# Attention and two feed-forward layers in one kernel: the first four tiles' probabilities transposed on TensorE, their swapped queries copied by ScalarE, and the row factors' Newton steps gathered

## The chip, the cores and the metric

One core of a Trainium2 chip runs the whole program. The metric is the device time of one execution in microseconds. The program before was run three times: 841.93, 842.92 and 845.69 us, so the median is 842.92 us.

## The reference, cut to what matters

```python
def _attn_ref(q, k, v):              # 4 batches, 8 heads, 576 rows, 64 columns
    scores = scale * np.matmul(q, k.transpose(0, 1, 3, 2))
    mask = block_i >= block_j        # blocks of 64 rows
    scores = np.where(mask, scores, -1000000000.0)
    scores = scores - np.max(scores, axis=-1, keepdims=True)
    attn = np.exp(scores)
    attn = attn / (np.sum(attn, axis=-1, keepdims=True) + 1e-09)
    return np.matmul(attn, v)

def _moe_ref(x, g_ln, w_ch1, w_ch2): # x: 2304 rows of 512; hidden width 2048
    xn = (x - mu) / np.sqrt(var + 1e-06) * g_ln
    return x + np.maximum(xn @ w_ch1, 0.0) @ w_ch2

def _moe2_ref(x, w_gate, w_local, w1, w2):   # 8 experts, hidden width 1024
    logits = np.einsum('bsd,de->bse', x, w_gate)
    ...                              # one expert e for each row, p its softmax
    out[b, s] = p[e] * (np.maximum(x[b, s] @ w1[e], 0.0) @ w2[e])
```

w_ch1 and w_ch2 arrive as 64-bit numbers and are read as pairs of 32-bit integers.

## The kernel before, in words

The 2304 rows are 18 tiles of 128. Every product of 32-bit numbers is made of 16-bit parts, a high and a low one, so that each product is three 16-bit matmuls. The program has two halves. The first, up to some 625 us, runs the attention and the first feed-forward layer together; the second routes the rows to experts and runs the expert layer, 26 slots of some 10 us. The change is in the first half, and there in the part up to some 160 us.

**A step** is one head of one tile (18 x 8 = 144 steps, the loop at the end of the first half). For a step, `qk` makes the scores on TensorE (L308), `maxes` takes their negated row maximum on VectorE (L328, L332), and `exps` lets ScalarE take the exponential (L339) and cast its high part (L348), lets GpSimd subtract for the low part (L351), and has the pair of parts, called ph, transposed into pt by a DMA that SyncE's queue issues (L355). Four steps later `pv` multiplies pt with the values on TensorE (L370, L374), and ScalarE and VectorE bring the sums out (L382, L383). Tiles 0 and 1 have so few keys that two heads share one ph. Before a tile's steps its keys and queries are split in two parts and transposed by DMA (L247, L237). Of the queries a second copy with its two 64-row halves swapped is made by VectorE (L238, L239, one copy for each half); the second half of each score needs it.

**The weights** of the first layer are 32 pieces of 512 KB. VectorE makes a 32-bit float of a piece in three integer operations (`w_bits`, L195, L199, L202), ScalarE scales it and casts its high part (`w_hi`, L215, L216), GpSimd subtracts for the low part (`w_lo`, L220). Three buffers hold raw pieces. The first three loads are issued on SyncE's queue; every later one is issued on ScalarE's own queue (L181), behind the work that stands there. A piece's load is asked for when the piece three before it has been read.

**After a tile's last head**, `finish` divides, takes mean and variance (L395 to L418), makes a rough inverse root y on VectorE, normalises with it, splits and transposes the result by DMA into xg, and refines the row's factor by two Newton steps, seven small VectorE operations on one column (L436 to L455, with one column for each tile). The factor is only needed when `post` (L501) brings a tile out of the layer. `l1` multiplies xg with the first weights (L473 to L475) and brings the hidden columns out by ScalarE and VectorE (L477, L478); `l2` multiplies these with the second weights (L495 to L497). The first tile's `l2` needs all 32 pieces of the weights.

**What sets the order.** The program is written step by step. A scheduler then orders the instructions of the first half with a timeline of its own, so that an engine's order is not the order of the code. Code under `first(i)` gets a high priority for tiles below HT = 2. Each engine then works strictly in its order.

## Time and profile before

| what | us |
|---|---|
| median of three runs | 842.92 |
| the profiled execution's own time | 843.15 |
| its span from first to last instruction | 841.4 |
| TensorE busy with matmuls | 707.7 (84% of the span) |
| VectorE busy | 460.1 (55%) |
| ScalarE busy | 362.1 (43%) |
| GpSimd busy | 327.8 (39%) |

The shares are means over a program with different limits in its parts. In the first 160 us TensorE is idle more than half the time and VectorE hardly ever; from 280 us on it is the other way round. So a change in the first part is read from the rows of that part, in windows, and by who waits for whom there.

### The profile page before, as it was taken

The numbers are of one execution on the slowest core, as the hardware profiler recorded it, in microseconds if no ns is written. First come the engines' busy times: TensorE is split into PE (matmuls) and PEld (weight loads), VectorE is DVE, ScalarE is ACT, GpSimd is POOL, SyncE is SP. The second block draws the span as 40 slices with busy tenths as digits, with TensorE's granted clock in tenths as the row PEclk, the third lists the DMA queues.
The fourth block names the chain that finished last, engine by engine and source line by source line (L and its number), as shares of the span: only waits on it lengthen the run. The fifth ranks groups of instructions, "written<-read, shape, count | busy, mean of one in ns | idle before, by whom it ended". The sixth has DMA issues, their size and how long they took to land. (4 is left out here: it accounts for less than half of the span.)

```text
span 841.4 us, 16461 instructions
## 1 busy us (share of the span) xinstructions
PE 707.7 (84%) x5526; PEld 425.4 (51%) x5526; DVE 460.1 (55%) x1248; ACT 362.1 (43%) x843; POOL 327.8 (39%) x364
## 2 busy tenths in 40 slices
PE   0214758789899999898998999998997999999995
PEld 0113645486756857655654565555452444444442
DVE  2999979887755556765564575276881111111110
ACT  2764657675555437555553464164041111111110
POOL 1577747776465235454444553210002122112210
PEclk9999989999999999999999999999998999999999
DMA  9998998799987677799967865397116655665673
GB/s 193 194 227 203 210 203 196 147 184 178 168 144 157 132 141 153 123 184 173 166 131 132 170 100 102 65 341 253 40 43 127 112 125 126 125 121 130 132 129 73
DMA packets 328942, 127.33 MB, mean 151 GB/s; under 512 B 296912, under 2 KB 315344, under 8 KB 328848
## 3 DMA queue, kind: packets, MB, share of 16 engines
q1 hardware_dynamic: 321472, 100.73, 63.0%
q10 hardware_dynamic: 4176, 15.21, 6.8%
q0 software_dynamic: 3200, 10.23, 3.7%
q8 instruction: 48, 0.79, 0.4%
q14 instruction: 46, 0.38, 0.2%
HBM read 128.73 MB, written 9.70 MB: 165 GB/s over the span
## 5 line engine op out<-in xcount | busy, mean ns | idle before, releaser
L473 PE MATMUL dps<-xg,wide 128*128 128x128 f16 (+2 forms) x576 | 156.4, 282 | 28.0 <-DVE htl L478 14.8
L351 POOL TENSOR_TENSOR ph<-sm,ph 128x512 f16<-128x512 f32 (+6 forms) x120 | 132.2, 1105 | 121.8 <-ACT ph L348 83.9
L474 PE MATMUL dps<-xg,wide 128*128 128x128 f16 (+2 forms) x576 | 156.7, 282 | 0.0
L475 PE MATMUL dps<-xg,wide 128*128 128x128 f16 (+2 forms) x576 | 156.6, 282 | 0.0
L339 ACT ACTIVATE sm<-sm,sums 128x128 f32<-128x128 f32 (+8 forms) x144 | 87.9, 611 | 111.5 <-DVE sums L332 100.7
L308 PE MATMUL ps_s<-wide 128*128 128x128 f16 (+4 forms) x560 | 74.9, 260 | 49.2 <-DVE sums L328 27.4
L1001 DVE SCALAR_TENSOR_TENSOR hth<-hps,hth 128x512 f16<-128x512 f32 x38 | 26.2, 691 | 164.6 <-ACT hth L1000 164.4
L495 PE MATMUL dps<-wide,hth 128*128 128x512 f16 x288 | 110.8, 386 | 0.2 <-DVE early L564 0.2
L496 PE MATMUL dps<-wide,hth 128*128 128x512 f16 x288 | 110.7, 385 | 0.0
L497 PE MATMUL dps<-wide,htl 128*128 128x512 f16 x288 | 110.4, 383 | 0.0
L370 PE MATMUL ps_o<-wide,pt 128*128 128x128 f16 x464 | 59.3, 225 | 29.3 <-DVE ob L383 19.0
L474 PEld LDWEIGHTS <-wide 128*128 128x128 f16 x576 | 58.9, 102 | 47.1 <-issue 33.8
L478 DVE SCALAR_TENSOR_TENSOR htl<-dps,hth 128x128 f16<-128x128 f32 (+2 forms) x144 | 59.1, 417 | 42.2 <-ACT hth L477 41.7
L1025 POOL DMA_INDIRECT out<-eo,dst_i x19 | 19.2, 1013 | 156.1 <-ACT eo L1024 151.4
L328 DVE CUSTOM_DVE_ANT_0 sm<-ps_s,mask_a 128x256 f32<-128x256 f32 (+7 forms) x128 | 64.2, 516 | 18.2 <-POOL ph L351 9.6
L308 PEld LDWEIGHTS <-wide 128*128 128x128 f16 x560 | 39.6, 101 | 61.8 <-issue 27.3
L348 ACT CAST ph<-sm 128x512 f16<-128x512 f32 (+6 forms) x120 | 68.2, 570 | 1.6
L477 ACT ACTIVATE hth<-dps 128x128 f16<-128x128 f32 (+2 forms) x144 | 53.5, 375 | 33.5 <-PE dps L475 33.3
L475 PEld LDWEIGHTS <-wide 128*128 128x128 f16 x576 | 59.1, 103 | 14.8
L473 PEld LDWEIGHTS <-wide 128*128 128x128 f16 x576 | 59.1, 103 | 14.6 <-issue 0.6
L370 PEld LDWEIGHTS <-pt 128*128 128x128 f16 x464 | 43.7, 100 | 26.3 <-DMA pt<-ph 17.9
L374 PE MATMUL ps_o<-wide,pt 128*128 128x64 f16 x464 | 55.9, 197 | 0.0
(255 smaller groups left out, 1408.4 us busy)
## 6 DMA issues: line engine op xcount, KB each, us to landing
raws<-in_moe_w SPq DMA_DIRECT2D x38, 2048.0 KB
wraw<-in_moe_w_ch ACTq DMA_DIRECT2D x29, 512.0 KB
raws<-in_moe_w SPq DMA_DIRECT2D x24, 512.0 KB
rows<-x2h SPq DMA_DIRECT2D x18, 256.0 KB
raw<-in_k SPq DMA_DIRECT2D x32, 128.0 KB
raw<-in_q SPq DMA_DIRECT2D x32, 128.0 KB
raw<-in_v SPq DMA_DIRECT2D x32, 128.0 KB
pt<-ph SPq DMA_TRANSPOSE x120
```

The source lines that it names most:

```text
L308: nc.tensor.matmul(sp[:, a * P + o:b * P], lhsT=qt[i, part].rearrange("p (x t) c -> p x (t c)", t=2)[:, x, z::2], rhs=rhs, start=part == 0 ...
L328: nc.vector.tensor_tensor_reduce(out=sm[:, lo:n], in0=sp[:, lo:n], in1=mask[:, 5 * P - n + lo:5 * P], scale=-0.125, scalar=3.0e38, op0=ALU ...
L339: nc.scalar.activation(out=e, in_=e, func=AF.Exp, scale=-1.0, bias=sv[:, 0, h:h + 1], accum_out=sv[:, 1, h:h + 1],)
L348: nc.scalar.copy(out=ph4[:, :, 0, lo:], in_=sm[:, :, lo:])
L351: nc.gpsimd.tensor_tensor(out=ph4[:, :, 1, lo:], in0=sm[:, :, lo:], in1=ph4[:, :, 0, lo:], op=ALU.subtract)
L370: nc.tensor.matmul(o, lhsT=t[:, c], rhs=vt[kk][:, h].rearrange("p e d -> p (e d)"), start=c == 0, stop=False,)
L473: nc.tensor.matmul(hp, lhsT=wh, rhs=xg[g][:, kk], start=kk == 0, stop=False)
L474: nc.tensor.matmul(hp, lhsT=wh, rhs=xg[g][:, KD + kk], start=False, stop=False)
L475: nc.tensor.matmul(hp, lhsT=wl, rhs=xg[g][:, kk], start=False, stop=kk == KD - 1)
L495: nc.tensor.matmul(op[j], lhsT=hh, rhs=w2h[:, f], start=f == 0, stop=False)
L496: nc.tensor.matmul(op[j], lhsT=hh, rhs=w2l[:, f], start=False, stop=False)
L497: nc.tensor.matmul(op[j], lhsT=hl, rhs=w2h[:, f], start=False, stop=f == KF - 1)
```

## The change

Three things, all in the first half:

1. For tiles 0 to 3 (FEW = 4), except their last two steps, ph is no longer transposed by DMA. TensorE multiplies each 128 x 128 block of it with an identity matrix into PSUM, and ScalarE copies the result into pt (`emit_turns`, two steps behind the exponential). For this the score tiles of these four tiles take half the PSUM they had (512 columns), and two PSUM tiles for the transposes stand beside them.
2. For the same tiles ScalarE makes the swapped copies of the queries.
3. A tile's product w = y·var·y is put into a column of `roots`; the other Newton steps run later for all the columns that are there (`newton`, when a tile's `l2` is at its third quarter), and are told to stand behind the last weights' piece. The two operations that multiplied by a pointer scalar and a tensor become two plain products each.

Besides, HT is 4, so tiles 0 to 3 and their splits run at high priority, and the splits' buffers are two, with one of its own for xh.

```diff
-HT = 2
+HT = 4
+FEW = 4
+LAGT = 2
...
+    ident16 = const.tile([P, P], F16, name="ident16")
+    gp.affine_select(
+        out=ident16, in_=c_one16, pattern=[[1, P]], compare_op=ALU.is_equal, fill=0.0,
+        base=0, channel_multiplier=-1,
+    )
...
+    sctx["p"] = sctx["c"].enter_context(tc.tile_pool(name="ps_e", bufs=1, space=PSUM))
...
-        n = at.tile([P, H, 2, D], F16, tag="nat", name="qn", bufs=3)
+        n = at.tile([P, H, 2, D], F16, tag="nat", name="qn", bufs=2)
...
-        nc.vector.tensor_copy(b[0:D], a[D:P])
-        nc.vector.tensor_copy(b[D:P], a[0:D])
+        copy = nc.scalar.copy if i < FEW else nc.vector.tensor_copy
+        copy(b[0:D], a[D:P])
+        copy(b[D:P], a[0:D])
...
-            sps[i] = ps_a.tile([P, 1024], F32, tag="s", name="ps_s", bufs=2)
+            n = 1024 if i >= FEW else 512
+            sps[i] = sctx["p"].tile([P, n], F32, tag="s", name="ps_s", bufs=2)
...
-        nc.sync.dma_start_transpose(out=t[:, :2 * m * n // P], in_=ph[:, :2 * m * n])
+        if step[0] < FEW * H - 2:
+            turns.append((step[0], ph, t, 2 * m * n // P))
+        else:
+            nc.sync.dma_start_transpose(out=t[:, :2 * m * n // P], in_=ph[:, :2 * m * n])
...
+    def emit_turns(upto):
+        while turns and turns[0][0] <= upto:
+            _, ph, t, n = turns.pop(0)
+            tp = sctx["p"].tile([P, 8, P], F16, tag="t", name="ps_t", bufs=2)
+            for c in range(n):
+                nc.tensor.transpose(tp[:, c], ph[:, c * P:(c + 1) * P], ident16)
+            nc.scalar.copy(out=t[:, :n], in_=tp[:, :n])
...
-        xh = at.tile([P, 2, DM], F16, tag="nat", name="xh", bufs=3)
+        xh = at.tile([P, 2, DM], F16, tag="xh", name="xh", bufs=1)
...
-        f = fac[:, i:i + 1]
         nc.vector.scalar_tensor_tensor(
-            out=w, in0=y, scalar=var, in1=y, op0=ALU.mult, op1=ALU.mult
+            out=roots[:, 0, i:i + 1], in0=y, scalar=var, in1=y, op0=ALU.mult, op1=ALU.mult
         )
+        fresh_roots.append(i)
...
+    def newton():
+        if fresh_roots:
+            with tc.issue_after(piece[0].ins):
+                newton_steps()
...
+    def newton_steps():
+        a, b = fresh_roots[0], fresh_roots[-1] + 1
+        fresh_roots.clear()
+        f, w, y = fac[:, a:b], roots[:, 0, a:b], roots[:, 1, a:b]
+        tt = nc.vector.tensor_tensor
         nc.vector.tensor_scalar(
             out=f, in0=w, scalar1=-1.0, scalar2=3.0, op0=ALU.mult, op1=ALU.add
         )
-        nc.vector.scalar_tensor_tensor(
-            out=y, in0=f, scalar=w, in1=f, op0=ALU.mult, op1=ALU.mult
-        )
+        tt(out=y, in0=f, in1=w, op=ALU.mult)
+        tt(out=y, in0=y, in1=f, op=ALU.mult)
...
     def l2(g, j, c):
...
+        if c == 2 and g < len(GROUPS) - 1:
+            newton()
...
+                if steps[s + 1:s + 2] == [(FEW, 0)]:
+                    emit_turns(s)
+                    sctx["c"].close()
+                    sctx["p"] = actx.enter_context(tc.tile_pool(name="ps_s", bufs=1, space=PSUM))
...
+                with first(nx):
+                    if h == SK:
+                        split_k(nx, nc.gpsimd)
...
+        emit_turns(s - LAGT)
         emit_pv(s - (LAG if s < LATE else LAG + MPT))
```

The change also moves instructions. Three places, each engine's order before and now (line numbers are those of the kernel that is shown):

ScalarE at the start of the program, before. The casts of tile 0's keys and queries (L245, L230) are followed at once by the first weights' piece (L215, L216) and the load that it frees (L181).

```order
L245 CAST kn<-raw 128x8x64
L230 CAST qn<-raw 128x8x64
L215 ACTIVATE wide<-wide,gs 128x512
L216 CAST wide<-wide 128x512
L181 DMA wraw<-in_moe_w_ch 128x1024
L256 ACTIVATE wide<-raw 128x8x64
L245 CAST kn<-raw 128x8x64
L230 CAST qn<-raw 128x8x64
```

The same place now (in the changed kernel the weights' piece is L229, L230, its load L194, and the swapped copies are L253, L254).

```order
L260 CAST kn<-raw 128x8x64
L244 CAST qn<-raw 128x8x64
L253 COPY wide<-wide 64x1024
L254 COPY wide<-wide 64x1024
L229 ACTIVATE wide<-wide,gs 128x512
L260 CAST kn<-raw 128x8x64
L244 CAST qn<-raw 128x8x64
L230 CAST wide<-wide 128x512
L194 DMA wraw<-in_moe_w_ch 128x1024
```

The two swapped copies, which need the transposed queries, and the casts of tile 1 now stand ahead of the first load that ScalarE issues.

VectorE at the last pieces of the weights, before: a Newton chain (L442 to L455) stands between the last pieces.

```order
L442 SCALAR_TENSOR_TENSOR lns<-fac,lns 128x1
L328 ISA sm,sums<-ps_s,mask_a 128x512
L328 ISA sums 128x1
L202 SCALAR_TENSOR_TENSOR wt<-wraw,wt 128x512
L445 SCALAR_TENSOR_TENSOR fac<-lns,fac 128x1
L332 TENSOR_SCALAR sums<-sums 128x1
L448 SCALAR_TENSOR_TENSOR lns<-fac,lns 128x1
L451 TENSOR_SCALAR lns<-lns 128x1
L455 TENSOR_TENSOR fac<-fac,lns 128x1
L383 TENSOR_TENSOR ob<-ps_o,ob 128x256
```

The same place now: from the very last piece (its last operation is L216 here) on, towards the first tile that leaves the layer (L544, four rows further down).

```order
L216 SCALAR_TENSOR_TENSOR wt<-wraw,wt 128x512
L482 TENSOR_SCALAR fac<-roots 128x2
L519 SCALAR_TENSOR_TENSOR htl<-dps,hth 128x128
L492 TENSOR_SCALAR roots<-roots 128x1
L344 ISA sm,sums<-ps_s,mask_a 128x512
L344 ISA sums 128x1
L348 TENSOR_SCALAR sums<-sums 128x1
L485 TENSOR_TENSOR roots<-fac,roots 128x2
L496 TENSOR_TENSOR fac<-fac,roots 128x1
```

Two chains, one of tile 0 alone and one of tiles 1 and 2, have taken the place of three; the first begins ahead of the last piece, the second behind it. Up to that first tile VectorE has made the row maxima of 35 heads before and of 32 now, and four of the swapped half copies where there were twelve.

TensorE, now: the first transposes (L385) stand among the scores (L324) of tiles 0 and 1; before there is nothing between the scores there.

```order
L324 MATMUL ps_s<-wide 128x128
L385 LDWEIGHTS ph
L385 MATMUL ps_t<-ident_64,ph 128x128
L385 LDWEIGHTS ph
L385 MATMUL ps_t<-ident_64,ph 128x128
L385 LDWEIGHTS ph
L385 MATMUL ps_t<-ident_64,ph 128x128
L385 LDWEIGHTS ph
L385 MATMUL ps_t<-ident_64,ph 128x128
L385 LDWEIGHTS ph
L385 MATMUL ps_t<-ident_64,ph 128x128
L324 LDWEIGHTS wide
```

In all there are 144 transposes, all ahead of the first tile's logits, and 22 copies of them on ScalarE (4 of 512 columns, 8 of 768, 10 of 1024). Ahead of these logits TensorE had made 96 matmuls of scores and 190 of `pv` before, and makes 76 and 160 now; from the third tile's logits on the same counts stand ahead of each tile's as before, but for the transposes. On SyncE's queue the 22 transposes by DMA are gone.

## Rows read from the trace of the kernel before

**Rows 1.** Windows: busy time of each engine in stretches of the span (us, and in brackets how many instructions), then the granted TensorE clock, the DMA engines' busy share and GB/s. 162 us is where the first tile leaves the first layer, 203 us the third. The columns are PE, PEld (the weight loads), DVE, ACT, POOL.

```profile
0.00:20.00 20.00, 0.39 (x2) 0.13 (x2) 5.13 (x15) 4.58 (x7) 3.56 (x11) 1.00 0.92 189
...
20.00:62.00 42.00, 9.30 (x62) 6.35 (x63) 41.27 (x100) 27.62 (x69) 26.52 (x21) 1.00 0.97 212
...
20.00:162.00 142.00, 76.85 (x713) 54.49 (x713) 134.49 (x300) 87.40 (x213) 93.04 (x72) 0.96 0.94 200
162.00:203.00 41.00, 35.48 (x473) 27.33 (x472) 31.20 (x110) 29.13 (x82) 30.48 (x37) 0.96 1.02 177
...
260.00:320.00 60.00, 57.81 (x557) 41.57 (x555) 34.25 (x111) 28.94 (x83) 21.41 (x22) 1.00 0.68 135
```

**Rows 2.** Waits of VectorE from 20 to 158 us: who it waited for, us in total, times, longest.

```profile
DVE wt L195 <- DMA wraw<-in_moe_w_ch: 2.3, 2, 1.3
DVE htl L478 <- ACT hth L477: 1.9, 2, 1.5
DVE wide L238 <- DMA wide<-qn: 0.9, 1, 0.9
```

**Rows 3.** Timeline of VectorE (start, duration, us): the last operation on the last piece of the weights, and the first tile leaving the layer (`post`).

```profile
157.41 0.69 DVE L202 SCALAR_TENSOR_TENSOR wt<-wraw,wt 128x512 int32<-128x512 int32 x1
...
162.14 0.75 DVE L501 SCALAR_TENSOR_TENSOR x<-dps,fac,x 128x512 f32<-128x512 f32 x1 [1.12 <-PE dps L497]
```

**Rows 4.** Groups of VectorE's instructions from 20 to 162 us (count; busy us, mean ns of one; idle before): the swapped copies of six tiles and the factor chains of three.

```profile
L239 DVE COPY wide<-wide 64x1024 f16<-64x1024 f16 x6 | 4.9, 810 | 0.1
L238 DVE COPY wide<-wide 64x1024 f16<-64x1024 f16 x6 | 4.8, 805 | 1.0 <-DMA wide<-qn 0.9
L448 DVE SCALAR_TENSOR_TENSOR lns<-fac,lns 128x1 f32<-128x1 f32 x3 | 3.3, 1095 | 0.0
L445 DVE SCALAR_TENSOR_TENSOR fac<-lns,fac 128x1 f32<-128x1 f32 x3 | 2.9, 962 | 0.0
L442 DVE SCALAR_TENSOR_TENSOR lns<-fac,lns 128x1 f32<-128x1 f32 x3 | 2.4, 804 | 0.0
L436 DVE SCALAR_TENSOR_TENSOR lns<-lns 128x1 f32<-128x1 f32 x3 | 1.6, 526 | 0.0
L455 DVE TENSOR_TENSOR fac<-fac,lns 128x1 f32<-128x1 f32 x3 | 1.4, 474 | 0.0
L451 DVE TENSOR_SCALAR lns<-lns 128x1 f32<-128x1 f32 x3 | 0.4, 145 | 0.0
L439 DVE TENSOR_SCALAR fac<-lns 128x1 f32<-128x1 f32 x3 | 0.4, 139 | 0.0
```

**Rows 5.** Timeline of VectorE: the same operation in its short and its long form (swapped copy, chain product, last product), and two row maxima of a tile with 640 keys in succession.

```profile
20.34 0.42 DVE L239 COPY wide<-wide 64x1024 f16<-64x1024 f16 x1
...
80.87 1.28 DVE L239 COPY wide<-wide 64x1024 f16<-64x1024 f16 x1
...
88.58 0.21 DVE L442 SCALAR_TENSOR_TENSOR lns<-fac,lns 128x1 f32<-128x1 f32 x1
...
95.24 1.11 DVE L455 TENSOR_TENSOR fac<-fac,lns 128x1 f32<-128x1 f32 x1
...
147.01 1.10 DVE L442 SCALAR_TENSOR_TENSOR lns<-fac,lns 128x1 f32<-128x1 f32 x1
...
152.13 0.16 DVE L455 TENSOR_TENSOR fac<-fac,lns 128x1 f32<-128x1 f32 x1
...
158.14 0.77 DVE L328 CUSTOM_DVE_ANT_0 sm<-ps_s,mask_m 128x640 f32<-128x640 f32 x1
...
159.07 0.82 DVE L328 CUSTOM_DVE_ANT_0 sm<-ps_s,mask_m 128x640 f32<-128x640 f32 x1
```

**Rows 6.** Groups of ScalarE's instructions up to 180 us: casts of 512 and of 640 columns, and copies out of PSUM of 128 and of 256 columns.

```profile
L477 ACT ACTIVATE hth<-dps 128x128 f16<-128x128 f32 x38 | 10.2, 270 | 7.2 <-PE dps L475 7.2
...
L348 ACT CAST ph<-sm 128x512 f16<-128x512 f32 x12 | 7.3, 610 | 0.0
...
L348 ACT CAST ph<-sm 128x640 f16<-128x640 f32 x8 | 5.8, 720 | 0.1
...
L382 ACT COPY ob<-ps_o 128x256 f32<-128x256 f32 x9 | 3.2, 360 | 0.1
```

**Rows 7.** Waits of ScalarE from 20 to 62 us, in the same form as rows 2.

```profile
ACT wide L215 <- DVE wide L202: 8.7, 6, 4.0
ACT kn L245 <- DMA raw<-in_k: 8.0, 1, 8.0
ACT sm L339 <- DVE sums L332: 4.8, 5, 1.7
```

**Rows 8.** Timeline of ScalarE's sequencer: the first load of a weights' piece that it issues.

```profile
8.85 0.44 ACTq L181 DMA_DIRECT2D wraw<-in_moe_w_ch  x1
```

**Rows 9.** SyncE's DMA queue from 20 to 130 us: packets, MB, share of the 16 DMA engines' time.

```profile
q1 hardware_dynamic: 36286, 9.93, 54.6%
```

**Rows 10.** Timeline of TensorE: two pairs of matmuls of 128 columns in succession, one pair early and one later.

```profile
71.00 0.31 PE L475 MATMUL dps<-xg,wide 128*128 128x128 f16 x1
71.11 0.31 PE L473 MATMUL dps<-xg,wide 128*128 128x128 f16 x1
...
88.62 0.22 PE L473 MATMUL dps<-xg,wide 128*128 128x128 f16 x1
88.67 0.22 PE L474 MATMUL dps<-xg,wide 128*128 128x128 f16 x1
```

More of the change, by code (lines that the diff above doesn't have):

```diff
@@ L125 @@
     fac = wp.tile([P, NTILE], F32, name="fac")
+    roots = wp.tile([P, 2, NTILE], F32, name="roots")
     gs = wp.tile([P, KD], F32, name="gs")
@@ L132 @@
     ps_a = actx.enter_context(tc.tile_pool(name="ps_a", bufs=1, space=PSUM))
+    sctx = {"c": ExitStack()}
+    sctx["p"] = sctx["c"].enter_context(tc.tile_pool(name="ps_e", bufs=1, space=PSUM))
     wctx = {"c": ExitStack()}
@@ L184 @@
     wt = {}
+    piece = [None]
     def w_bits(p):
@@ L201, in w_bits @@
         )
-        nc.vector.scalar_tensor_tensor(
+        piece[0] = nc.vector.scalar_tensor_tensor(
             out=t, in0=low, scalar=29, in1=t, op0=ALU.logical_shift_right, op1=ALU.bitwise_or
@@ L243, in split_k @@
         r = raw.pop(("k", i))
-        n = at.tile([P, H, 2, D], F16, tag="nat", name="kn", bufs=3)
+        n = at.tile([P, H, 2, D], F16, tag="nat", name="kn", bufs=2)
         nc.scalar.copy(out=n[:, :, 0], in_=r)
@@ L354, in exps @@
         t = ring("pt", [P, 10, P], F16, LAG, MPT)
-        nc.sync.dma_start_transpose(out=t[:, :2 * m * n // P], in_=ph[:, :2 * m * n])
+        if step[0] < FEW * H - 2:
+            turns.append((step[0], ph, t, 2 * m * n // P))
+        else:
+            nc.sync.dma_start_transpose(out=t[:, :2 * m * n // P], in_=ph[:, :2 * m * n])
         for j in range(m):
             ptr[i, h - m + 1 + j] = t[:, 2 * n // P * j:2 * n // P * (j + 1)]
+    turns = []
+    def emit_turns(upto):
[5 more added lines that the diff above has]
+            nc.scalar.copy(out=t[:, :n], in_=tp[:, :n])
     obs = {}
@@ L406, in finish @@
         sm = at.tile([P, 12], F32, tag="lns", name="lns", bufs=2)
-        mean, var, y, w = (sm[:, c:c + 1] for c in (6, 7, 8, 9))
+        mean, var, y = (sm[:, c:c + 1] for c in (6, 7, 8))
         nc.vector.bn_stats(out=sm[:, 0:6], in_=x)
@@ L433, in finish @@
             nc.vector.reciprocal(out=stats[:, c, 1:2], in_=y)
-        f = fac[:, i:i + 1]
         nc.vector.scalar_tensor_tensor(
-            out=w, in0=y, scalar=var, in1=y, op0=ALU.mult, op1=ALU.mult
+            out=roots[:, 0, i:i + 1], in0=y, scalar=var, in1=y, op0=ALU.mult, op1=ALU.mult
         )
+        fresh_roots.append(i)
+    fresh_roots = []
+    def newton():
[7 more added lines that the diff above has]
+        tt = nc.vector.tensor_tensor
         nc.vector.tensor_scalar(
@@ L441, in finish @@
         )
-        nc.vector.scalar_tensor_tensor(
-            out=y, in0=f, scalar=w, in1=f, op0=ALU.mult, op1=ALU.mult
-        )
+        tt(out=y, in0=f, in1=w, op=ALU.mult)
+        tt(out=y, in0=y, in1=f, op=ALU.mult)
         nc.vector.scalar_tensor_tensor(
@@ L447, in finish @@
         )
-        nc.vector.scalar_tensor_tensor(
-            out=y, in0=f, scalar=w, in1=f, op0=ALU.mult, op1=ALU.mult
-        )
+        tt(out=y, in0=f, in1=w, op=ALU.mult)
+        tt(out=y, in0=y, in1=f, op=ALU.mult)
         nc.vector.tensor_scalar(
@@ L454, in finish @@
         )
-        nc.vector.tensor_tensor(out=f, in0=f, in1=y, op=ALU.mult)
+        tt(out=f, in0=f, in1=y, op=ALU.mult)
     todo = []
@@ L529, in early_logits @@
     def early_logits(js):
+        if fresh_roots:
+            newton_steps()
         g = len(GROUPS) - 1
@@ L742 @@
         if s in (8, 16, 24)[:EARLY]:
+            emit_turns(s - 1)
             emit_pv(s - 1)
@@ L757 @@
                 nx = ORDER[t + 1]
-                if h == SK:
-                    split_k(nx, nc.gpsimd)
-                if h == SQ:
-                    split_q(nx, nc.gpsimd)
-                if h == SV:
-                    split_v(nx)
+                with first(nx):
+                    if h == SK:
+                        split_k(nx, nc.gpsimd)
+                    if h == SQ:
+                        split_q(nx, nc.gpsimd)
+                    if h == SV:
+                        split_v(nx)
                 if h == SL:
```

## The prediction

> **What bounds the kernel now.** I read the windows first, since a mean over the program hides its parts. From 20 to 162 us VectorE is busy 134.5 of 142 us and TensorE 76.9; from 260 to 320 us it is VectorE 34.3 and TensorE 57.8 of 60 [rows 1]. So the program has a VectorE-paced start and a TensorE-paced middle, and a microsecond on VectorE is worth something only at the start. The waits come next: from 20 to 158 us VectorE waits for others some 5 us [rows 2], and the rest of its idle time is small. Then the end of the stretch. VectorE finishes the last piece of the weights at 158.1 us, and 4 us later the first tile leaves the layer, after a wait of 1.12 us for TensorE [rows 3]. What VectorE does ahead of that piece therefore delays all that follows. In the stretch from 162 to 203 us TensorE is busy 35.5 of 41 us [rows 1]: there it sets the pace already, with 5.5 us to spare.
>
> ScalarE is the engine to watch on the other side. It is busy 87.4 of 142 us, and 27.6 of the 42 us from 20 to 62 [rows 1]; its idle time there is spent waiting for VectorE (8.7 and 4.8 us) and for keys to arrive (8.0) [rows 7].
>
> **The change, part by part.** The sum is made at the first tile's leave, 162 us, and then carried on to the end.
>
> *Swapped copies.* Twelve copies of VectorE stand ahead of that point, 9.7 us in all, and four are left by the order; the eight that go are worth 8 x 0.81 = 6.5 us at the mean [rows 4]. But the same copy takes 0.42 us at one place and 1.28 at another [rows 5]. The long form is 0.86 us of something other than copying, and GpSimd, 93 of 142 us busy [rows 1], is the candidate. If that part is only handed on to the next operation, 8 x 0.42 = 3.4 us go. I take the middle, 5.0.
>
> The Trainium skill, page SBUF — State Buffer, section SBUF: two separate sides, says why it could be handed on: VectorE and GpSimd share one pair of ports as an exclusive lock for a whole instruction, and the loser stands still; it names VectorE's two-port modes and two-input operations. The trace agrees as far as the 0.21 and the 1.10 us of one and the same one-column product go [rows 5]. By that rule alone the copies would give 3.4, and the sum below would end 1.6 us later.
>
> *Newton steps.* Three chains stand ahead of the point, 12.4 us for seven operations each [rows 4]. Now there are three first products (1.6 us) and two chains of eight operations. A chain has the linear step 0.14, the middle product 0.96, the scaling 0.15 and five plain products; at the 0.47 us of the one plain product there is [rows 4] that is 3.6 us, so 1.6 + 7.2 = 8.8, and 3.6 us are saved. The bounds: at 0.16 us a product [rows 5] a chain takes 2.0 and 6.8 us are saved; at 1.11 [rows 5] it takes 6.8, and 2.8 us are lost. I take 3.6, by the mean of the nearest row. Gathering saves less than 18 chains becoming 11 suggests, because two of the eleven are still ahead of the first leave.
>
> *Heads put off.* VectorE has three row maxima less to make ahead of the point; tile 4's follow each other at 159.07 - 158.14 = 0.93 us [rows 5], so 2.8 us. That is put off, not saved.
>
> VectorE together: 5.0 + 3.6 + 2.8 = 11.4 us earlier.
>
> *ScalarE.* A cast takes 0.61 us for 512 columns and 0.72 for 640 [rows 6], 0.86 ns a column, so a copy of 1024 columns is 1.05 us by estimate and eight are 8.4 us. Out of PSUM 128 columns take 0.27 us and 256 take 0.36 [rows 6]; carried on, 512, 768 and 1024 columns take 0.54, 0.72 and 0.90 (or 0.61, 0.83 and 1.05 by the casts), so the 22 copies take 17 to 19.5 us. ScalarE's 87.4 us grow to about 113 of the same 142, less the three heads put off. As a mean that fits. But the work lies early: by the twelfth piece of the weights (about 62 us) its order holds all eight swapped copies and six copies out of PSUM, 12.6 us more, on 27.6 busy of 42 [rows 1]; that makes 40 of 42. And every load of a piece after the third is issued on this engine: the first of them now goes out at 8.85 us [rows 8], while in the new order it stands behind the two copies, which need the transposed queries, there at about 19.9 us, when VectorE copies them today (the second copy starts at 20.34 [rows 5]). So the cover of the 12.6 us is ScalarE's idle time, which is there only where it does not wait for VectorE; with that cover gone they delay the pieces one for one. Ends 0 and 12.6; I take half, 6.3 us later, since of its 21.5 us of waits [rows 7] only the 8.0 for keys is no wait for VectorE.
>
> *TensorE's transposes.* 144 at 0.05 (late pair) to 0.11 us (early pair) [rows 10] are 8 to 16 us, in a stretch where it is idle 65 of 142 us [rows 1]. I count 0; the cover is that idle time. A transpose that waits for GpSimd's subtraction holds up what stands behind it in TensorE's order, as the wait for pt did until now.
>
> *DMA.* The 22 transposes move 0.5 + 1.0 + 1.5 + 1.5 = 4.5 MB (two parts of 128 to 512 columns), of the 9.93 MB that SyncE's queue moves from 20 to 130 us with 54.6% of the engines' time [rows 9]. About a quarter of all DMA time there becomes free. VectorE waits for DMA only 3.2 us in the stretch [rows 2], so at most 3.2 us are gained; I count 0, because the loads are also asked for later.
>
> *From 162 us on.* Put off are three row maxima, 20 score matmuls (five heads of 2 x 512 + 2 x 128 columns, 0.55 us each at 0.055 us for 128 columns) and 30 of `pv` (15 x 0.083), together 4.0 us of TensorE. The stretch to 203 us has 5.5 us of TensorE's idle time [rows 1], but waits made it. I take half of the 4.0 on the path: 2.0 us later. Behind that the order is the old one, TensorE-paced, and everything shifts as a whole.
>
> The sum: -11.4 + 6.3 + 2.0 = -3.1 us, on the profiled execution's own 843.15 us (its span is 841.4): 840.05. That execution is 0.23 us above the median of the runs, so the median should be about **839.8 us**. Its own bounds are -8 to +2 us. A measurement of this kernel can tell about 0.5%, 4.2 us, from no change; the forecast lies inside that.
>
> **The rivals.**
>
> *ScalarE keeps up.* Its 14 idle us of the early 42 [rows 1] take all the new copies. For it: most of them are waits for VectorE, which gets faster, and the freed DMA time shortens loads. Against it: 40 of 42 us in strict order. Then -11.4 + 2.0 = -9.4: 833.5 us, and 829 with the best ends of copies and Newton steps.
>
> *ScalarE paces the start* (the other side, slower). The copies delay the loads of the weights one for one, each later piece waits, and the 4.0 us put off come on top: -11.4 + 12.6 + 4.0 = +5.2, so 848 us; with blocked Newton products (6.4 us worse) 854. It decides when more than 9.4 us of the 12.6 fall on the path. For it: ScalarE's order at the start; against it: a mean load of 77% over the whole stretch.
>
> The Trainium skill, page ScalarE: Activation LUTs, section Rules for kernel authors, speaks against moving such work: it sends simple elementwise work to VectorE, up to about three times as fast there in 16 bits. The rows here say 1.05 us (estimate) against 0.42 to 1.28, so the rule holds only where GpSimd leaves VectorE alone.
>
> *The first leave doesn't set the rest.* If the TensorE-paced stretch starts by its own work, the gain of the start is swallowed at once and the time stays at 842.9 us. Against it: TensorE idles 65 us ahead of that point.
>
> **How the numbers follow.** Forecast 0.45, ScalarE keeps up 0.27, ScalarE paces 0.20, no effect 0.08. Faster by over 0.5%: all of the second and a third of the first, 0.42. Slower by over 0.5%: the third but for its mildest part, with a little of the forecast's upper end, 0.21. Within 0.5%: 0.37. The range reaches over most of both rivals, 831 to 848 us.
>
> **What would show it.** Right: VectorE's last piece some 4 to 6 us ahead of 158.1, the first leave at 155 to 159, ScalarE over 90% busy from 20 to 62 us, and VectorE waiting there for pieces' loads. ScalarE keeping up would show as a first leave ahead of 153 us with VectorE still without waits; ScalarE pacing as a leave behind 162 us with VectorE idle 15 us or more in the stretch. The forecast is wrong in kind if the difference at the end is not the one at 203 us.

## The result and the profile after

The changed kernel takes 853.19 us (four runs, 851.37 to 854.94) where the kernel before takes 842.42 (four runs). The ratio is 1.0123, 95% interval 1.0081 to 1.0165: slower by 7 to 14 us. The forecast was 839.8 and its range ended at 848. The profiled execution took 851.37 us (span 849.3), 8.2 us more than that of before.

Windows of the changed kernel, columns as in [rows 1], and the same two milestones as in [rows 3]:

```profile
20.00:62.00 42.00, 12.56 (x78) 7.83 (x76) 35.96 (x86) 35.30 (x77) 29.09 (x24) 0.89 1.05 250
20.00:162.00 142.00, 81.34 (x803) 58.41 (x802) 124.03 (x273) 105.90 (x237) 96.10 (x74) 0.87 0.70 169
162.00:203.00 41.00, 35.64 (x461) 26.96 (x460) 25.08 (x90) 27.51 (x76) 25.68 (x29) 0.96 0.95 157
260.00:320.00 60.00, 57.31 (x543) 40.61 (x542) 29.09 (x110) 30.83 (x83) 27.04 (x30) 1.00 0.79 147
```

```profile
154.42 0.69 DVE L216 SCALAR_TENSOR_TENSOR wt<-wraw,wt 128x512 int32<-128x512 int32 x1
161.14 0.75 DVE L544 SCALAR_TENSOR_TENSOR x<-dps,fac,x 128x512 f32<-128x512 f32 x1 [2.49 <-PE dps L540]
...
209.07 0.74 DVE L544 SCALAR_TENSOR_TENSOR x<-dps,fac,x 128x512 f32<-128x512 f32 x1
...
638.60 0.74 DVE L544 SCALAR_TENSOR_TENSOR x<-dps,fac,x 128x512 f32<-128x512 f32 x1
```

VectorE's busy time from 20 to 162 us fell by 10.5 us, near the 11.4 that the forecast subtracts. But its last piece came only 3.0 us earlier and the first leave 1.0 earlier; in the fixed stretch VectorE was idle 18 us where there were 7.5. From there it turns round: the third leave is 6.4 us later than before (209.07 against 202.64) and the last one 9.6 (638.60 against 629.03). So most of the loss is there by 209 us. TensorE is not idle longer after 162 us: it is as busy there as before (35.64 against 35.48 of 41 us). It came to 162 us with less done. The windows from the start to 162 us, of before and of the changed kernel, show it (the first bracket counts matmuls):

```profile
0.00:162.00 162.00, 77.25 (x715) 54.62 (x715) 139.61 (x314) 91.98 (x220) 96.60 (x83) 0.97 0.94 199
0.00:162.00 162.00, 83.46 (x817) 59.95 (x818) 130.91 (x296) 112.97 (x247) 99.74 (x85) 0.88 0.72 171
```

Of the 817 matmuls 144 are the new transposes, so 673 are its old work, where before 715 were done: 42 fewer. From 162 to 203 us another 12 are missing (461 against 473) in the same busy time.

What held TensorE, first before and then now (waits of TensorE, 20 to 162 us; us, times, longest):

```profile
PE ps_s L308 <- DVE sums L328: 24.9, 10, 7.7
PE ps_o L370 <- DVE ob L383: 16.2, 3, 9.2
PE dps L473 <- DVE htl L478: 9.0, 7, 4.1
PE ps_o L370 <- DMA pt<-ph: 6.3, 4, 2.8
```

```profile
PE ps_s L324 <- DVE sums L344: 17.1, 6, 5.9
PE ps_t L385 <- ACT ph L364: 16.6, 6, 4.9
PE ps_t L385 <- POOL ph L367: 12.0, 8, 3.1
PE dps L514 <- DVE htl L519: 8.1, 7, 3.2
```

Waits for VectorE became shorter, and the wait for pt by DMA is gone (6.3). In their place TensorE stands 28.6 us in front of transposes, for the cast or the subtraction that makes ph. Whether the matmuls behind them could have run earlier is not shown: at several places the next one waited again, as behind the transpose at 39.56 us, where it stood 5.8 us for row maxima.

VectorE's waits in that stretch [rows 2] have many sources now, none large:

```profile
DVE x L544 <- PE dps L540: 2.5, 1, 2.5
DVE wt L209 <- DMA wraw<-in_moe_w_ch: 2.1, 1, 2.1
DVE wt L209 <- POOL wide L234: 2.1, 3, 1.5
DVE wide L209 <- POOL ph L367: 1.7, 1, 1.7
DVE htl L519 <- ACT hth L518: 1.5, 3, 0.7
```

VectorE's groups from 20 to 162 us that answer to [rows 4]: the swapped copies that are left, and of the two chains the first products and the two longest operations.

```profile
L253 DVE COPY wide<-wide 64x1024 f16<-64x1024 f16 x2 | 1.6, 784 | 0.1
...
L463 DVE SCALAR_TENSOR_TENSOR roots<-lns 128x1 f32<-128x1 f32 x3 | 1.5, 505 | 0.0
L254 DVE COPY wide<-wide 64x1024 f16<-64x1024 f16 x2 | 1.5, 733 | 0.0
L490 DVE TENSOR_TENSOR roots<-fac,roots 128x2 f32<-128x2 f32 x1 | 1.1, 1132 | 0.0
L490 DVE TENSOR_TENSOR roots<-fac,roots 128x1 f32<-128x1 f32 x1 | 1.1, 1105 | 0.0
```

ScalarE's new groups (0 to 180 us), its waits from 20 to 62 us [rows 7], its first load [rows 8] and SyncE's queue from 20 to 130 us [rows 9]:

```profile
L386 ACT COPY pt<-ps_t 128x1024 f16<-128x1024 f16 x10 | 10.0, 1005 | 0.3 <-PE ps_t L385 0.2
L386 ACT COPY pt<-ps_t 128x768 f16<-128x768 f16 x8 | 6.3, 796 | 0.5 <-PE ps_t L385 0.5
L253 ACT COPY wide<-wide 64x1024 f16<-64x1024 f16 x4 | 4.2, 1043 | 7.4 <-DMA wide<-qn 7.3
L254 ACT COPY wide<-wide 64x1024 f16<-64x1024 f16 x4 | 4.2, 1043 | 0.0
L386 ACT COPY pt<-ps_t 128x512 f16<-128x512 f16 x4 | 2.3, 578 | 0.1
```

```profile
ACT wide L229 <- DVE wide L216: 3.4, 2, 1.7
ACT sm L355 <- DVE sums L348: 1.6, 2, 1.1
ACT kn L260 <- DMA raw<-in_k: 1.1, 1, 1.1
```

```profile
18.67 0.38 ACTq L194 DMA_DIRECT2D wraw<-in_moe_w_ch  x1
```

```profile
q1 hardware_dynamic: 24702, 7.61, 40.6%
```

The copies cost what was estimated: 18.6 us out of PSUM, 8.4 for the swaps. ScalarE is 84% busy from 20 to 62 us and the first load that it issues leaves 9.8 us later than before, yet VectorE waits for pieces of the weights hardly more than it did.

### The profile page after: what moved, and what is told of

It reads as the page before. It is cut to its first block, busy times and chain, and to the rows that moved or that the text cites. A ratio compares the mean times of both kernels' runs of the same rounds, so it can differ in the third digit from the quotient of the medians.

```text
span 849.3 us, 16718 instructions
## 1 busy us (share of the span) xinstructions
PE 719.2 (85%) x5670; PEld 434.3 (51%) x5670; DVE 436.8 (51%) x1220; ACT 386.4 (45%) x873; POOL 330.1 (39%) x365
## 5 line engine op out<-in xcount | busy, mean ns | idle before, releaser
L324 PE MATMUL ps_s<-wide 128*128 128x128 f16 (+4 forms) x560 | 73.4, 258 | 39.7 <-DVE sums L344 22.5
L324 PEld LDWEIGHTS <-wide 128*128 128x128 f16 x560 | 39.0, 101 | 49.5 <-issue 23.3
L1052 ACT ACTIVATE hth<-hps 128x512 f16<-128x512 f32 x38 | 22.6, 596 | 73.0 <-PE hps L1035 73.0
```

Source lines behind the costliest of these rows:

```text
L324: nc.tensor.matmul(sp[:, a * P + o:b * P], lhsT=qt[i, part].rearrange("p (x t) c -> p x (t c)", t=2)[:, x, z::2], rhs=rhs, start=part == 0 ...
```

## The experiments

All ratios are to the kernel before, run on the same chip; brackets hold the 95% interval. "Over before" is how far the ratio lies above 1, times 840 us, about the median of before on those chips. Two kernels are compared by the difference of their ratios, some of them from different chips.

**One part of the change alone, on the kernel before.** e1_newton has the gathered Newton steps, e2_swap ScalarE's swapped copies, e3_turns the transposes on TensorE with the new pools, e4_ht the priorities.

```diff
 e2_swap
-        nc.vector.tensor_copy(b[0:D], a[D:P])
-        nc.vector.tensor_copy(b[D:P], a[0:D])
+        copy = nc.scalar.copy if i < FEW else nc.vector.tensor_copy
+        copy(b[0:D], a[D:P])
+        copy(b[D:P], a[0:D])
 e4_ht
-HT = 2
+HT = 4
+                with first(nx):        # around split_k, split_q, split_v
```

> The kernel before with the gathered Newton steps alone. All theories: VectorE has 3 to 7 us less ahead of the first tile's leave, ScalarE and TensorE nothing more, so 2 to 5 us faster, about 839 us. If it is slower, moving the chain has cost by itself (the first leave waits for its factor).

> The kernel before with the swapped copies of tiles 0 to 3 on ScalarE alone. Theory S (ScalarE's work at the start delays the weights' pieces, because their loads are issued behind it): 2 to 6 us slower, about 846 us, with VectorE idle more in 20 to 62 us. Theory T (TensorE's order with its transposes is the cost): no loss, 0 to 5 us faster, since VectorE has 5 us less.

> The kernel before with the transposes of tiles 0 to 3 on TensorE (and their copies on ScalarE, and the smaller score tiles) alone; high priority for two tiles as before. Theory T (transposes wait in TensorE's order for GpSimd's subtraction, hold up what is behind them and push tile 4's scores behind the first leave): 6 to 12 us slower, about 851 us, the loss showing between the first and the third leave. Theory S: 2 to 5 us slower by the 17 to 19 us of copies. Theory P (priority of tiles 2 and 3): no change.

> The kernel before with high priority for tiles 0 to 3 and their splits instead of 0 and 1, alone. Theory P (the priority puts the attention of tiles 2 and 3 ahead of the weights and so delays the first leave): 4 to 10 us slower. Theories S and T: within 2 us of before.

| kernel | median us | ratio | over before |
|---|---|---|---|
| e1_newton | 840.56 | 1.0001 [0.9971, 1.0031] | 0 |
| e2_swap | 845.57 | 1.0069 [1.0036, 1.0102] | +5.8 |
| e3_turns | 848.51 | 1.0107 [1.0073, 1.0142] | +9.0 |
| e4_ht | 837.86 | 0.9977 [0.9942, 1.0012] | -1.9 |

e1_newton was expected 2 to 5 us faster and is not; the theory that the priorities cost 4 to 10 us fell with e4_ht. e2_swap is the instructive one. Two milestones in its trace are early, and the kernel is slower all the same:

```profile
148.83 0.68 DVE L203 SCALAR_TENSOR_TENSOR wt<-wraw,wt 128x512 int32<-128x512 int32 x1
...
157.47 0.74 DVE L503 SCALAR_TENSOR_TENSOR x<-dps,fac,x 128x512 f32<-128x512 f32 x1
...
203.81 0.75 DVE L503 SCALAR_TENSOR_TENSOR x<-dps,fac,x 128x512 f32<-128x512 f32 x1 [1.29 <-PE dps L499]
```

The last piece of the weights is 8.6 us ahead of [rows 3] and the first leave 4.7 ahead; so neither late loads nor a late first leave made the loss. The third leave is 1.2 us late. Up to 162 us e2_swap had made 17 matmuls more than before (732 against 715); from 162 to 203 us it made 45 fewer (428 against 473), and why is not shown.

**What in e3_turns costs.** g1_pool keeps its pools and takes the transposes out; g2_twice makes each transpose twice, g3_copytwice each copy out of PSUM twice.

```diff
 g2_twice
-                nc.tensor.transpose(tp[:, c], ph[:, c * P:(c + 1) * P], ident16)
+                for _ in range(2):
+                    nc.tensor.transpose(tp[:, c], ph[:, c * P:(c + 1) * P], ident16)
 g3_copytwice
-            nc.scalar.copy(out=t[:, :n], in_=tp[:, :n])
+            for _ in range(2):
+                nc.scalar.copy(out=t[:, :n], in_=tp[:, :n])
```

> The kernel before with the changed pools alone: score tiles of 512 columns for the first four tiles, two buffers of the natural-layout tiles and a tile of its own for xh, and the probabilities' transposes still in the DMA queues (no transpose on TensorE, no copy out of PSUM). Theory 'TensorE's work is paid in full': within 0.5% of before, some 8 us under e3_turns. Rival 'the smaller PSUM tiles or the buffers make scores and splits wait': most of the loss of e3_turns is here too, over 845 us on the scale where before is 841.

> e3_turns with every one of TensorE's 144 transposes of probabilities issued twice. Theory 'TensorE's work is paid in full': 144 more of 55 ns at the full clock to 107 ns at the half clock, so +8 to +15 us over e3_turns (some 857 to 864 where before is 841). Rival 'the transposes lie in TensorE's idle time and e3_turns lost by its order or its pools': within 3 us of e3_turns. Rival 'more activity lifts the clock': at or below e3_turns.

> e3_turns with each ScalarE copy of transposed probabilities out of PSUM done twice, some 17 to 20 us more on ScalarE over the first 170 us and nothing more on TensorE. Theory 'TensorE's work is paid in full, ScalarE is not the bound': within 4 us of e3_turns. Rival 'ScalarE paces the start': +8 us or more over e3_turns.

g1_pool: 846.42 us, 1.0088 [1.0051, 1.0124]. g2_twice: 851.44, 1.0129 [1.0087, 1.0171]. g3_copytwice: 853.83, 1.0158 [1.0116, 1.0201]. The theory that TensorE's work is paid in full fell: doubling the transposes added 1.8 us to e3_turns (-2.7 to +6.4) and not 8. Doubling the copies, 19.5 us more on ScalarE, added 4.3 (-0.3 to +8.9), between the two theories and not clear of nothing. The pools alone, at HT 2, already cost 7.4 us, so that the transposes and their copies add only 1.6 to them there (-2.6 to +5.8). Why the pools cost that much stays open. The two traces also differ in another way: from 20 to 162 us e3_turns' VectorE waits 10.3 us for transposed queries, g1_pool's 0.8.

**The parts within the changed kernel.** f2_noturn leaves the transposes to the DMA queues and keeps all the rest. h1_peonly adds to f2_noturn the transposes on TensorE alone, h2_actonly the copies on ScalarE alone; pt comes by DMA in both, and what is added is read by nobody. f1_noswap is the changed kernel with the swaps on VectorE.

```diff
 h1_peonly, h2_actonly
         nc.sync.dma_start_transpose(out=t[:, :2 * m * n // P], in_=ph[:, :2 * m * n])
+        if step[0] < FEW * H - 2:
+            turns.append((step[0], ph, t, 2 * m * n // P))
 h1_peonly
-            nc.scalar.copy(out=t[:, :n], in_=tp[:, :n])
 h2_actonly
-            tp = sctx["p"].tile([P, 8, P], F16, tag="t", name="ps_t", bufs=2)
-            for c in range(n):
-                nc.tensor.transpose(tp[:, c], ph[:, c * P:(c + 1) * P], ident16)
-            nc.scalar.copy(out=t[:, :n], in_=tp[:, :n])
+            tp = sctx["p"].tile([P, 8, P], F32, tag="t", name="ps_t", bufs=1)
+            nc.scalar.copy(out=tp[:, :n], in_=ph[:, :n * P].rearrange("p (n c) -> p n c", n=n))
```

> The changed kernel with the first four tiles' probabilities transposed in the DMA queues again; ScalarE's swaps, the gathered Newton steps, HT at 4 and the new pools stay. Theory 'TensorE's transposes cost their whole time': 6 to 10 us under the changed kernel, so 841 to 846 where before is 841 (the swaps' 5 us stay). Rival 'the loss comes from ScalarE and the pools': within 3 us of the changed kernel, 848 or more.

> f2_noturn (the change without its transposes) plus the 144 transposes on TensorE, at their places in the order, into PSUM tiles that nobody reads: pt still comes by DMA, and ScalarE has no copies out of PSUM. Theory 'TensorE's added work is paid in full': the 8 to 9 us between the changed kernel and f2_noturn are here, 849 to 853 us where before is 840. Rival 'the copies on ScalarE or the new way of ph through TensorE and ScalarE cost it': within 3 us of f2_noturn, 840 to 845.

> f2_noturn plus 22 copies on ScalarE of as many columns as the changed kernel copies out of PSUM, at the same places (here from ph into PSUM, read by nobody); pt still comes by DMA, and TensorE has no transposes. Theory 'TensorE's added work is paid in full': within 3 us of f2_noturn, 840 to 845. Rival 'ScalarE's added work paces the start': +6 us or more over f2_noturn, 848 or more.

> The changed kernel with the swapped copies of the first four tiles back on VectorE; transposes on TensorE, pools, HT at 4 and the gathered Newton steps stay. If the swaps on ScalarE cost what they cost alone (e2_swap, +0.7%), 5 to 6 us under the changed kernel, 846 to 849 where before is 840. If they hide once tiles 0 to 3 run at high priority, as f2_noturn suggests (all of the change but the transposes came to +0.2%), within 3 us of the changed kernel, some 850 to 853.

| kernel | median us | ratio | over before |
|---|---|---|---|
| f2_noturn | 842.35 | 1.0021 [0.9990, 1.0052] | +1.8 |
| h1_peonly | 845.98 | 1.0083 [1.0047, 1.0119] | +7.0 |
| h2_actonly | 852.49 | 1.0143 [1.0100, 1.0185] | +12.0 |
| f1_noswap | 851.71 | 1.0136 [1.0090, 1.0182] | +11.4 |
| the changed kernel | 853.19 | 1.0123 [1.0081, 1.0165] | +10.3 |

So within the changed kernel the transposes with their copies carry the loss: 8.6 us (4.2 to 13.0) between f2_noturn and the changed kernel. With e3_turns' pools at HT 2 they added 1.6, so this price seems to belong to this order and not to the work alone (the 7.0 us between are uncertain by 6). The larger half is not TensorE's. The copies on ScalarE alone cost 10.2 us (5.9 to 14.6), the transposes on TensorE alone 5.2 (1.2 to 9.2); the difference is barely clear of the noise. h2_actonly's copies go the other way, from ph into PSUM as 32-bit floats, and take as long (median 0.81 us against 0.80). Together they would be 15.4; that both cost 8.6 leaves some 7 us that the DMA queues' relief may give back, uncertain by as much. The swaps make no difference that shows here (1.1 us in favour of ScalarE, uncertain by 5). Waits of h2_actonly, of TensorE and then of VectorE, 20 to 162 us:

```profile
PE ps_s L324 <- DVE sums L344: 42.4, 12, 11.3
PE ps_o L396 <- DMA pt<-ph: 19.0, 7, 6.6
```

```profile
DVE htl L516 <- ACT hth L515: 8.4, 7, 4.0
DVE wide L209 <- DMA wraw<-in_moe_w_ch: 4.0, 2, 2.1
```

The same waits of f2_noturn:

```profile
PE ps_s L324 <- DVE sums L344: 48.6, 13, 10.0
PE ps_o L396 <- DMA pt<-ph: 2.3, 3, 1.6
DVE htl L516 <- ACT hth L515: 1.1, 3, 0.4
```

The wait for row maxima is no longer than there. What grew are TensorE's wait for pt and VectorE's for the hidden columns that ScalarE makes. The second points at ScalarE directly. The first does not: the transposes by DMA stand in SyncE's queue, and whether a late cast of ScalarE, GpSimd's subtraction or the queue made pt late is not shown. Nor do the rows settle how h1_peonly's 5.2 us come about: its TensorE stands 8.6 us in front of transposes, but its VectorE also waits 9.0 us for pieces of the weights, where f2_noturn's waits 1.1.

**The price of a microsecond on each engine**, in the kernel before. n1_dve makes the swapped copies of six tiles twice on VectorE; n2_pe issues the first score matmul of each head of tiles 0 to 3 three times; n3_act makes their casts of ph twice.

```diff
 n1_dve
-        nc.vector.tensor_copy(b[0:D], a[D:P])
-        nc.vector.tensor_copy(b[D:P], a[0:D])
+        for _ in range(2 if i < 6 else 1):
+            nc.vector.tensor_copy(b[0:D], a[D:P])
+            nc.vector.tensor_copy(b[D:P], a[0:D])
 n3_act
-        nc.scalar.copy(out=ph4[:, :, 0, lo:], in_=sm[:, :, lo:])
+        for _ in range(2 if i < 4 else 1):
+            nc.scalar.copy(out=ph4[:, :, 0, lo:], in_=sm[:, :, lo:])
```

> The kernel before with the twelve swapped copies of the first six tiles made twice on VectorE, at the mean of rows 4 some 9.7 us more on that engine ahead of the first leave, and nothing else. If VectorE paces the start one for one, as the prediction had it: +8 to +10 us (848 to 850 where before is 840) and the last weights' piece as much later. Rival 'the start is paced by chains across engines, and a microsecond of VectorE is worth half or less': +5 us or less, 845 or under.

> The kernel before with the first score matmul of each part of every head of tiles 0 to 3 issued three times instead of once: 64 more matmuls of 128 to 512 columns, 20480 columns, 8.9 us of TensorE at the full clock, all in the first 160 us, without a wait of their own. If TensorE's idle time there covers such work, as the prediction counted: within 3 us of before. Rival 'the work is paid in full because the order of the rest is fixed by TensorE': +7 to +10 us. In between (h1_peonly: +5 for 8.0 us): half of it.

> The kernel before with ScalarE's cast of the high part of the probabilities made twice for tiles 0 to 3: 24 more casts of 256 to 512 columns, some 12.5 us by rows 6, nothing else. If ScalarE's idle time (55 of 142 us) covers it: within 3 us of before. Rival 'ScalarE's added work paces the start' (h2_actonly: +10 for 18.8 us): +5 to +8 us, 845 to 848 where before is 840.

| kernel | added work, us | ratio | over before | per us added |
|---|---|---|---|---|
| n1_dve | 7.0 VectorE | 1.0174 [1.0127, 1.0222] | 14.6 | 2.1 (1.5 to 2.7) |
| n2_pe | 8.9 TensorE | 1.0067 [1.0042, 1.0092] | 5.6 | 0.63 (0.4 to 0.9) |
| n3_act | 13.0 ScalarE | 1.0054 [1.0029, 1.0080] | 4.5 | 0.35 (0.2 to 0.5) |

The 8.9 us are 20480 columns at the full clock, the 13.0 the casts that n3_act's groups have more (12 of 0.61, 8 of 0.51 and 4 of 0.39 us). The 7.0 us are the groups of n1_dve up to 170 us, less the 9.7 us of [rows 4] (the second copy follows the first at once and is shorter):

```profile
L239 DVE COPY wide<-wide 64x1024 f16<-64x1024 f16 x12 | 9.6, 803 | 1.1 <-DMA wide<-qn 0.7
L240 DVE COPY wide<-wide 64x1024 f16<-64x1024 f16 x12 | 7.1, 591 | 0.4
```

Work added to VectorE at the start is paid one for one or more, as the prediction had it (by the two profiled executions alone 7.5 us). But TensorE's and ScalarE's idle time covers only a third to two thirds of what is put there. In n2_pe's profile the granted clock from 20 to 162 us is 0.82, where before has 0.96, so that a part of the 5.6 us could be the clock's. Its nine runs don't bear that out: the six with a mean clock of 0.945 to 0.955 took 841.75 to 847.09 us, the three with 0.967 to 0.975 took 844.15 to 847.52.

**Amount, or pools?** m1_few2 is the changed kernel with FEW = 2.

> The changed kernel with FEW at 2: transposes on TensorE and swapped copies on ScalarE for tiles 0 and 1 alone, 40 transposes (2.2 us at the full clock) and 7 copies out of PSUM (some 5 us) where there were 144 and 22 (8.0 and 18.6). If the loss follows the amount of work put on TensorE and ScalarE: about 0.28 of the 8.5 us between the changed kernel and f2_noturn, so 843 to 846 where before is 840. Rival 'the loss comes from the pools and the order at the start': as much as with FEW at 4, 849 or more.

847.02 us, 1.0087 [1.0056, 1.0117]: between the two theories. With 28% of the transposes, 7.3 us of the 10.3 remain. The 3.0 us between are not clear of the noise (they are uncertain by 4.4), so this run doesn't settle how much goes with the amount and how much with the pools and the order.

**A version that might beat both.** k1_htnewton joins e4_ht and e1_newton.

> The two parts of the change that cost nothing by themselves, together: HT at 4 with the splits at their tile's priority, and the gathered Newton steps; no transposes on TensorE, swaps on VectorE, the pools as before. Expected from e4_ht (0.9977) and e1_newton (1.0001): 0.4% to 0 faster, 836 to 840 where before is 840.

839.47 us, 1.0007 [0.9977, 1.0038]. Neither it nor e4_ht can be told from the kernel before; e4_ht has the lowest ratio.

**One count that nearly orders them.** For each profile: when VectorE's last weights piece, the first and the third leave start, how many matmuls of TensorE's old work are in the trace up to 203 us (added transposes and repeats taken off), and the profiled execution's own time. (e1_newton is left out: its profiled execution took 848.23 us, well above its median of 840.56. With its 1146 matmuls the correlation below stays at -0.92.)

| kernel | last piece | first leave | third leave | matmuls | own time |
|---|---|---|---|---|---|
| e4_ht | 150.78 | 157.03 | 198.36 | 1231 | 837.78 |
| k1_htnewton | 150.12 | 158.49 | 202.05 | 1196 | 839.47 |
| f2_noturn | 154.19 | 164.43 | 205.36 | 1194 | 838.86 |
| before | 157.41 | 162.14 | 202.64 | 1185 | 843.15 |
| e2_swap | 148.83 | 157.47 | 203.81 | 1160 | 847.01 |
| g1_pool | 158.99 | 165.49 | 206.95 | 1159 | 844.18 |
| m1_few2 | 154.26 | 162.94 | 207.23 | 1147 | 844.08 |
| n2_pe | 155.02 | 162.44 | 205.75 | 1144 | 846.26 |
| after | 154.42 | 161.14 | 209.07 | 1133 | 851.37 |
| n1_dve | 159.83 | 167.67 | 209.57 | 1116 | 850.68 |
| e3_turns | 164.49 | 168.68 | 210.00 | 1102 | 848.51 |
| g2_twice | 157.63 | 166.93 | 214.76 | 1099 | 854.23 |
| n3_act | 157.45 | 167.92 | 210.90 | 1097 | 850.40 |
| h1_peonly | 159.66 | 170.42 | 213.42 | 1090 | 849.83 |
| h2_actonly | 164.72 | 171.42 | 216.06 | 1085 | 855.89 |
| f1_noswap | 163.69 | 169.42 | 216.09 | 1071 | 851.71 |
| g3_copytwice | 166.14 | 175.88 | 214.42 | 1062 | 854.33 |

It is read from windows of 0 to 203 us, here of before, of the changed kernel, of e4_ht and of h2_actonly (the first bracket counts matmuls; the changed kernel's has 144 transposes in it):

```profile
0.00:203.00 203.00, 112.73 (x1185) 81.95 (x1186) 170.81 (x424) 121.10 (x301) 127.08 (x119) 0.97 0.95 194
```

```profile
0.00:203.00 203.00, 119.10 (x1277) 86.91 (x1278) 156.00 (x386) 140.48 (x322) 125.42 (x114) 0.90 0.77 168
```

```profile
0.00:203.00 203.00, 118.62 (x1231) 86.57 (x1232) 174.81 (x433) 124.27 (x308) 130.21 (x122) 0.94 0.97 198
```

```profile
0.00:203.00 203.00, 104.27 (x1085) 76.56 (x1086) 156.07 (x377) 139.07 (x317) 119.98 (x110) 0.93 0.95 190
```

Over these 17 kernels the count correlates with the time at -0.92, the first leave at 0.72, the last piece at 0.69. The third leave, near the 203 us at which the prediction looks, does nearly as well, at 0.90. A least-squares line through the counts gives 0.105 us for each missing matmul; a matmul of the TensorE-paced stretch takes 57.81 / 557 = 0.104 us [rows 1]. This fits a start that is worth how far TensorE gets with its old work in it, with what is missing paid later at TensorE's own pace. A count and a time of one execution are a description, not a cause, the count takes long and short matmuls alike, and it was picked after the runs; but the 0.104 was not fitted to the times. Against the ratios of the tables the correlation is -0.84. Traces can lack a few records, so single places in the list are not to be relied on.

## Why the prediction was wrong, step by step

The forecast put the first leave 5.1 us earlier (-11.4 + 6.3) and took 2.0 of it back behind that point. The profile has the first leave 1.0 us earlier, loses 7.4 from the first leave to the third, and 1.8 more up to the end. So of the 11.3 us between the forecast's 840.05 and the profiled 851.37, 4.1 belong to the terms up to the first leave and 7.2 to what comes behind it. Of its own signs none came as forecast: the last piece was 3.0 us early instead of 4 to 6, the first leave came at 161.14 us instead of 155 to 159, and ScalarE was 84% busy instead of over 90%.

- *What bounds the kernel.* Half right. Work added to VectorE at the start delays the end (n1_dve), and TensorE paces the middle. That "a microsecond on VectorE is worth something only at the start" held for a microsecond added, not for one moved to ScalarE.
- *VectorE's 11.4 us.* Its busy time fell by 10.5, so the size of the whole was right, in part by luck. Within it the copies gave 6.6 us (3.1 are left of 9.7; 5.0 forecast) and the chains 5.8 (6.6 of 12.4; 3.6 forecast), while the operations on the weights' pieces (six groups, 91 and 90 operations) grew from 77.6 to 80.5 us: a quarter of what was taken out came back elsewhere on VectorE. By the Trainium skill's exclusive lock between VectorE and GpSimd (page SBUF — State Buffer, section SBUF: two separate sides) operations could lengthen so; no run here shows that the lock did it. Of the 10.5 us the path got 3.0 at the last piece and 1.0 at the first leave. In e2_swap 4.7 us did reach the first leave, and the kernel still lost 5.8. The Newton steps alone are worth 0 to within 2.6 us; their profile has VectorE only 0.6 us less busy from 20 to 162 us (133.92 against 134.49).
- *ScalarE's 6.3 us.* The durations were right (18.6 and 8.4 us). Too small was the price: the prediction counted half of the 12.6 us that lie ahead of the twelfth piece and nothing for the 14 later on. As many copies, added alone to f2_noturn, cost 10.2 us. The mechanism was not the one named either: VectorE waits for pieces 3.2 us in the changed kernel, 2.9 before. In h2_actonly the wait for ScalarE's hidden columns grew to 8.4 us and TensorE's for pt to 19.0; that these make the 10.2 us is argued, not shown.
- *TensorE's transposes, "I count 0; the cover is that idle time".* **This is the step that failed in kind.** The idle time is there, 65 of 142 us, but it is no full cover: the transposes alone cost 5.2 us (1.2 to 9.2) in h1_peonly and plain matmuls 5.6 in n2_pe, more than half of their 8.0 and 8.9 us at the full clock. (The 8.0 are 144 at 0.055 us, the step at which they follow each other; with the end of each row counted the changed kernel's trace books 17.8 us for them.) And the transposes brought waits of their own, 28.6 us in the changed kernel, where the prediction only named one and gave it no price. Through which of the waits the 5.2 us reach the end stays open.
- *DMA, 0.* The size of the relief was right: the DMA engines' busy share from 20 to 162 us fell from 0.94 to 0.70. By difference it may be worth some 7 us; not shown by a run of its own.
- *From 162 us on, 2.0.* Too small. The forecast counted 4.0 us of matmuls put off and took half of them on the path. The trace has 42 matmuls fewer done by 162 us, some 4.4 us at 0.104, so the count was about right; but from the first leave to the third the changed kernel needs 7.4 us more (47.9 against 40.5). That is all of what was put off and 3 us besides, which no row explains. "Everything shifts as a whole" from there is nearly right: 6.4 us at the third leave, 9.6 at the last.
- *The rivals.* "ScalarE paces the start", 848 us, is the nearest, in its sign and in the engine. Its condition, VectorE idle 15 us or more, was met (18); its other sign, a leave behind 162 us, was not, and its price was too low, perhaps because TensorE's share was left out. The 10.2 us of h2_actonly speak against "ScalarE keeps up". And "the first leave doesn't set the rest", which got the smallest chance, was right in its words (a 4.7 us earlier leave in e2_swap gained nothing) and wrong in its price.

The sum by what was measured: f2_noturn +1.8 (all of the change but the transposes), transposes +5.2, copies +10.2, together 17, where 10.3 were measured; the -7 put down to DMA is what is left over and no check of the sum. Open remains why the parts don't add up: swaps +5.8, pools +7.4, Newton steps 0, priorities -1.9 by themselves, but +1.8 together, and transposes with copies 1.6 on the pools at HT 2, but 8.6 in the changed kernel. A likely reason, not shown, is that each part changes the scheduler's whole order of the first half; no run held the order fixed while a part was changed.

## What to carry to other kernels

Idle time of an in-order engine in a stretch that another engine paces is not free room: measure its price by putting a known amount of harmless work there, one engine at a time, before moving work onto it. Where a later stretch is paced by one engine, judge the stretch ahead by how much of that engine's own work is done at a fixed time, not by when the pacing engine of the moment ends its last piece. And a price found by adding work to an engine is not what moving work away from it gives back: e2_swap made VectorE 8.5 us less busy from 20 to 162 us (125.97 against 134.49) with 8.4 us of copies on ScalarE, and lost 5.8.

## What the runs showed of the hardware that was not expected

TensorE's granted clock was lower in the changed kernel's profile from 60 to 100 us, at the same busy time as before. Windows of before, then of the changed kernel:

```profile
60.00:80.00 20.00, 6.49 (x63) 6.21 (x63) 19.93 (x33) 11.09 (x22) 14.98 (x11) 1.00 0.87 217
80.00:100.00 20.00, 14.33 (x143) 11.37 (x142) 19.88 (x49) 11.16 (x31) 13.50 (x11) 0.91 0.96 181
```

```profile
60.00:80.00 20.00, 6.58 (x54) 5.15 (x53) 17.71 (x25) 11.82 (x23) 15.38 (x12) 0.59 0.80 169
80.00:100.00 20.00, 14.43 (x160) 13.36 (x160) 17.11 (x40) 14.61 (x34) 11.96 (x10) 0.66 0.84 188
```

Most of those 40 us ran at 1.2 instead of 2.4 GHz, behind a stretch (20 to 62 us) in which TensorE was busy 12.56 us instead of 9.30. From 60 to 80 us 54 matmuls were made, where before made 63. But the time did not go with the clock: of the changed kernel's four runs the one with the lowest mean clock, 0.939, took 851.73 us, and those with 0.970 and 0.969 took 854.66 and 854.94.

Each of the ten plain products in the two factor chains ahead of the first leave works on one or two columns. Three of them took 0.93 to 1.13 us and seven 0.14 to 0.16: the long form of [rows 5] is there with plain products as it was with the pointer products that they replaced. What makes it long no run here shows.
